# Two projections of a chunk in one visit of the matrix engine, the second result held in SBUF

## The chip, the cores and the metric

The kernel runs on one core of a Trainium2 chip. A core has a matrix engine (TensorE; PE in the rows, PEld for its weight loads), VectorE (DVE), ScalarE (ACT), GpSimd (POOL), and a queue engine (SP) that starts DMA transfers. PE writes only to PSUM, a small memory of eight banks; DVE and ACT read PSUM and SBUF. Each engine takes its instructions strictly in the order in which the program lists them. The metric is the device time in microseconds of one execution.

## The reference

Three stages follow each other: an attention through 32 packed tokens per head, a mixture of 4 experts, and a last two-layer block.

```python
def sm_attn(qq, kk, vv):
    s = scale * np.matmul(qq, kk.transpose(0, 1, 3, 2))
    ...                                   # softmax over the last axis
    return np.matmul(a, vv)
p_packed = sm_attn(p, k, v)               # 4 batch, 8 heads, 32 packed, 64
out = sm_attn(q, p_packed, p_packed)      # 4 batch, 8 heads, 576 tokens, 64
x = out.transpose(0, 2, 1, 3).reshape(2304, 512)
p = domain_probs / (domain_probs.sum(-1, keepdims=True) + 1e-09)
for e in range(4):
    h = np.maximum(x @ w1[e], 0.0)        # 512 -> 1024
    out += p[:, e:e + 1] * (h @ w2[e])    # 1024 -> 512
h = x @ w_in                              # 512 -> 2048
return (h - np.tanh(h)) @ w_out
```

## The kernel before

**What a projection is.** The attention's output x is a product a2 · p_packed, where a2 holds the second softmax (8 heads x 32 packed = 256 numbers per token). So x @ w1 is computed as a2 · (p_packed @ w1). The inner product p_packed @ w1 is the *packed projection* (`pack_w1`, line 528): for one batch element and one chunk of the hidden layer it gives a 256 x 512 weight matrix, by which the 576 tokens of that batch element are then multiplied.

**Tiling.** The expert stage works in two passes `p` over two batch elements each (1152 tokens, 9 tiles of 128). In a pass it goes through 8 chunks `c` (expert c // 2, 512 of its 1024 hidden columns). Per chunk and batch element `bi` there are:

- one projection on PE: 8 matmuls of 64 x 32 weights and 512 columns into the PSUM tile `wps` (line 533); they use the array as eight small tiles side by side. Each is fp32 and is recorded as two passes, so 16 matmul rows in the trace;
- its sums (lines 545 to 557, shared between ACT and DVE): `wps` is split into a high and a low part, and five linear combinations of its quarters are formed in the tile `wsum` and split too. The result `wp` holds seven slots, high and low;
- seven products on PE (`up_prod`, line 612) in four steps, a Winograd scheme, into two PSUM tiles called X and Z (`hpx` and `hpz`, matmuls on line 628); DVE adds (`done`, line 639) and ACT copies (`kept`, line 635) combine them into the hidden values `h0`, `h1` (high and low parts, lines 564 and 565).

The down-projection (`down`, line 670, PSUM tile `yps`, matmuls on line 678) of the hidden values of one token tile is placed between the steps of the products.

**The order.** PE's and SP's orders are written out by hand as strings of tokens; DVE's and ACT's are set by a scheduler at build time. For each chunk there is an *even half* (`EVEN`, products of the first batch element, `g...0` to `g...3`, with five down-projections `d` of the chunk before between them) and an *odd half* (`ODD`, products of the second, with four). In the kernel before, each half ends with one projection for the next chunk: token `W..0` at the end of the even half, `W..1` at the end of the odd half. Background tokens `_` decode the last stage's 64-bit weights on ACT, DVE and POOL at the same time (tiles `f64`, `fo`, `fh`; fetched by SP, line 387).

**Buffers.** `wps` has one buffer of two PSUM banks (pool `psw`). X and Z share two such buffers (pool `ps2`). The raw weights of a chunk come by DMA as two tiles `wraw` (tokens `a0..0` and `a0..1` at the start of the even half), in a pool of two; a reload waits until the projections of the chunk before have read them. `wsum` shares a pool of five with the decoding tiles.

Of the kernel before, what the change touches and what calls it, by code (L numbers as in the profile page):

```python
# [9 lines left out]
F32 = mybir.dt.float32  # L10
F32R = mybir.dt.float32r
U32 = mybir.dt.uint32
ACTF = mybir.ActivationFunctionType
# [57 lines left out]
)  # L71

FIRST = (
    "d005 g1000 Q10 J10 R10 d006 g1001 b10 Q11 J11 R11 L3 d007 a020 a021 g1002 b11 g1003 W200 d008 "
    "g1010 d100 Q12 J12 R12 g1011 d101 Q13 J13 R13 g1012 d102 Q14 J14 R14 k10 k11 a120 a121 g1013 W201 b20 b21 d103 "
)

EVEN = (
    "d%(l)d%(p)d4 _ g%(c)d%(p)d00 a0%(e)d0 a0%(e)d1 _ k%(c)d0 d%(l)d%(p)d5 _ g%(c)d%(p)d01 d%(l)d%(p)d6 _ "
    "k%(c)d1 g%(c)d%(p)d02 _ d%(l)d%(p)d7 g%(c)d%(p)d03 W%(e)d%(q)d0 _ d%(l)d%(p)d8 "  # L80
)

ODD = (
    "g%(c)d%(p)d10 a1%(e)d0 _ d%(c)d%(p)d0 _ g%(c)d%(p)d11 b%(e)d0 _ d%(c)d%(p)d1 a1%(e)d1 _ g%(c)d%(p)d12 "
    "d%(c)d%(p)d2 g%(c)d%(p)d13 W%(e)d%(q)d1 _ d%(c)d%(p)d3 b%(e)d1 _ "
)

LASTA = (
# [21 lines left out]
def kernel(  # L110
# [13 lines left out]
    nc = tc.nc  # L124
# [6 lines left out]
    def pool(name, bufs=1, stack=None, **kw):  # L131
        return (stack or ctx).enter_context(
            tc.tile_pool(name=name, bufs=bufs, **kw, **({} if kw.get('space') == DRAM else {'reuse_waits': 'tile'}))
        )
# [14 lines left out]
    ps2 = pool("ps2", 2, pps, space=PSUM)  # L149
# [17 lines left out]
    psw = []  # L167
# [4 lines left out]
    def k4t(shape, dt, name):  # L172
        return p_k4.tile(shape, dt, tag="k", name=name)
# [8 lines left out]
    def f(ap):  # L182
        return ap.bitcast(F32)
# [119 lines left out]
    def q_scores(p, t0):  # L303
# [20 lines left out]
        sc3 = sc[:, 0:n].rearrange("p (g k) -> p g k", k=32)  # L324
        nc.vector.tensor_reduce(out=mx[:, 0:G, 0], in_=sc3, op=ALU.max, axis=AX.X)
        a2s[p, t0] = n, G, sc3, mx
# [11 lines left out]
    def q_norm(p, t0):  # L338
        a2, a23, G = a2s[p, t0]
        sm = small.tile([128, 16, 1], F32, tag="qsm", name="qsm")  # L340
        nc.vector.tensor_reduce(out=sm[:, 0:G, 0], in_=a23, op=ALU.add, axis=AX.X)
        nc.vector.tensor_scalar(
# [147 lines left out]
    w2h, w2l, wph, wpl, raw, w2s, unsaved = {}, {}, {}, {}, {}, {}, {}  # L490
# [33 lines left out]
    def save_w2(c, g):  # L524
        for k, t in enumerate(unsaved.pop((c, g), ())):
            nc.sync.dma_start(out=w2s[c, g][:, k], in_=f(t))

    def pack_w1(c, p, bi):
        ps = (psw[0] if psw else ps2).tile([128, 2, 512], F32, tag="pw" if psw else "p2", name="wps")
        for j in range(4):  # L530
            for r in range(2):
                d = slice(64 * r, 64 * r + 64)
                nc.tensor.matmul(  # L533
                    out=ps[32 * j:32 * j + 32, r, :],
                    lhsT=ppbd[p][d, bi, j, 32 * r:32 * r + 32], rhs=raw[0, c, j // 2][d, j % 2, :],
                )
        if c == 0:
            w = p_wp.tile([128, 2, 2, 512], F32R, tag="wp", name="wp")
            h, l = wph[c, p, bi], wpl[c, p, bi] = w[:, 0], w[:, 1]
            nc.scalar.activation(out=h, in_=ps, func=ACTF.Copy)  # L540
            nc.vector.tensor_tensor(out=l, in0=ps, in1=f(h), op=ALU.subtract)
            return
        w = p_wp.tile([128, 2, 7, 256], F32R, tag="wp", name="wp")
        h, l = wph[c, p, bi], wpl[c, p, bi] = w[:, 0], w[:, 1]
        s = k4t([128, 4, 256], F32, "wsum")
        a11, a12, a21, a22 = ps[:, 0, 0:256], ps[:, 1, 0:256], ps[:, 0, 256:512], ps[:, 1, 256:512]
        nc.scalar.activation(out=h[:, 0:2], in_=ps[:, :, 0:256], func=ACTF.Copy)
        nc.scalar.activation(out=s[:, 3], in_=a21, func=ACTF.Copy)
        nc.vector.tensor_tensor(out=l[:, 0:2], in0=ps[:, :, 0:256], in1=f(h[:, 0:2]), op=ALU.subtract)
        nc.scalar.activation(out=h[:, 2], in_=a22, func=ACTF.Copy)  # L550
        nc.vector.tensor_tensor(out=s[:, 0], in0=a22, in1=s[:, 3], op=ALU.add)
        nc.vector.tensor_tensor(out=l[:, 2], in0=a22, in1=f(h[:, 2]), op=ALU.subtract)
        nc.vector.tensor_tensor(out=s[:, 1], in0=s[:, 0], in1=a11, op=ALU.subtract)
        nc.vector.tensor_tensor(out=s[:, 2], in0=a11, in1=s[:, 3], op=ALU.subtract)
        nc.vector.tensor_tensor(out=s[:, 3], in0=a12, in1=s[:, 1], op=ALU.subtract)
        nc.scalar.activation(out=h[:, 3:7], in_=s, func=ACTF.Copy)
        nc.vector.tensor_tensor(out=l[:, 3:7], in0=s, in1=f(h[:, 3:7]), op=ALU.subtract)
# [4 lines left out]
    def split_h(fp, d, src):  # L562
        hi, lo = ht[fp]
        last[1] = nc.scalar.activation(out=hi[:, :, d], in_=src, func=ACTF.Relu).ins
        last[0] = nc.vector.scalar_tensor_tensor(
            out=lo[:, :, d], in0=src, scalar=0.0, in1=f(hi[:, :, d]), op0=ALU.max, op1=ALU.subtract,
        ).ins

    def up(c, p, un):
        bi, t0, n = UN[un]  # L570
        if not ht:
            ht.extend([p_h.tile([128, 2, TP * 128], F32R, name=f"h{fp}{s}") for s in "hl"] for fp in range(2))
        for fp in range(2):
            ps = ps2.tile([128, 2, 512], F32, tag="p2", name="hps")
            for ff in range(2):
                c0 = 128 * (2 * fp + ff)
                k = 0
                for g in range(2):
                    for a, x in ((wph, a2h), (wph, a2l), (wpl, a2h)):
                        nc.tensor.matmul(  # L580
                            out=ps[:, ff, 0:n],
                            lhsT=a[c, p, bi][:, g, c0:c0 + 128],
                            rhs=x[p][:, g, t0:t0 + n],
                            start=(k == 0), stop=(k == 5),
                        )
                        k += 1
            split_h(fp, slice(t0, t0 + n), ps[:, :, 0:n])
# [24 lines left out]
    def up_prod(c, p, bi, step):  # L612


        W, t0 = (wph[c, p, bi], wpl[c, p, bi]), bi * S_LEN
        A, T = (a2h[p], a2l[p]), (th[p], tl[p])

        def tok(g, half):
            return [x[:, g, t0 + half * HB:t0 + half * HB + HB] for x in A]

        def cmb(k):
            return [x[:, bi, k] for x in T]

        def mul(ps, slot, x, start, stop):
            for ff in range(2):
                c0 = slice(128 * ff, 128 * ff + 128)
                for k, (a, b) in enumerate(((0, 0), (0, 1), (1, 0))):
                    nc.tensor.matmul(  # L628
                        out=ps[:, ff, 0:HB], lhsT=W[a][:, slot, c0], rhs=x[b],
                        start=(start and k == 0), stop=(stop and k == 2), skip_group_check=True,  # L630
                    )

        def kept(ps, name):
            t = p_ct.tile([128, 2, HB], F32, tag="ct", name=name)
            last[1] = nc.scalar.activation(out=t, in_=ps[:, :, 0:HB], func=ACTF.Copy).ins
            return t

        def done(ps, t, fp, half):
            nc.vector.tensor_tensor(out=t, in0=ps[:, :, 0:HB], in1=t, op=ALU.add)  # L639
            split_h(fp, slice(t0 + half * HB, t0 + half * HB + HB), t)  # L640

        if step == 0:
            X = ps2.tile([128, 2, 512], F32, tag="p2", name="hpx")
            Z = ps2.tile([128, 2, 512], F32, tag="p2", name="hpz")
            mul(X, 0, tok(0, 0), True, False)
            t = kept(X, "p1")
            mul(Z, 1, tok(1, 0), True, True)
            done(Z, t, 0, 0)
            prod[bi] = [X, Z]
        elif step == 1:  # L650
            X, Z = prod[bi]
            mul(X, 4, cmb(1), False, False)
            prod[bi].append(kept(X, "u2"))
            mul(Z, 3, cmb(0), True, False)
            prod[bi].append(kept(Z, "p5"))
        elif step == 2:
            X, Z, u, p5 = prod[bi]
            mul(X, 5, cmb(2), False, False)
            done(X, p5, 1, 1)
            mul(Z, 6, tok(1, 1), False, True)  # L660
            done(Z, u, 0, 1)
        else:
            X = prod.pop(bi)[0]
            mul(X, 2, cmb(3), False, True)
            split_h(1, slice(t0, t0 + HB), X[:, :, 0:HB])
# [257 lines left out]
    def late_norm():  # L923
# [24 lines left out]
        "J": lambda p, i: q_exp(p, 2 * i),  # L948
        "k": save_w2,
        "W": pack_w1,  # L950
        "u": lambda c, p, i: up(c, p, ("u0", "m0", "m1", "u3")[i]),
        "d": down,
        "g": up_prod,
        "C": comb,
        "q": x_quad,
# [279 lines left out]
```

## Time and profile before

| | |
|---|---|
| median of 3 runs (lowest, highest) | 1070.21 us (1069.99, 1071.28) |
| the profiled execution, its own time | 1069.74 us |
| its span, first to last instruction | 1068.0 us |
| chain that ended last, share of PE | 90% |
| of it matmuls of `yps` / `ops` / `h3ps` | 33% / 19% / 16% |
| of it `hpx` / `hpz` / `wps` | 7% / 6% / 3% |

A busy time is the time in which an engine works on at least one instruction; a row of a timeline gives start and duration of one instruction or of several equal ones. Matmuls overlap in their pipeline, so what one costs is the distance from its start to the start of the next, not its duration. A wait names the engine and the instruction that ended it.

### The profile page before, as it was taken

Reading aid. Unit: us, or ns where it says so; the run is one execution under the profiler, and the core shown is the slowest. Engines: PE = TensorE matmul, PEld = TensorE weight load, DVE = VectorE, ACT = ScalarE, POOL = GpSimd, SP = SyncE. Lnnn points to the kernel's source line nnn. Section 1 sums busy time; section 2 is a strip of 40 time slices with the busy share of each in tenths; the row PEclk is TensorE's granted clock in tenths of the full one; section 3 lists DMA queues with packets and bytes.
Section 4 is the critical chain, followed back from the end, with each engine's and each line's share of the span. In section 5 each row is a group of like instructions: output and inputs, shape, how many; then the busy total and the mean of one; then the engine's idle time right before and its main releaser. Section 6 shows DMA issues by size and latency. Waiting matters only on the chain.

```text
span 1068.0 us, 16484 instructions
## 1 busy us (share of the span) xinstructions
PE 1055.8 (99%) x6344; PEld 898.7 (84%) x6344; DVE 884.1 (83%) x1353; ACT 623.9 (58%) x986; POOL 160.4 (15%) x122
## 2 busy tenths in 40 slices
PE   8999999999999999999999999999999999999998
PEld 6777888888888888888888888889999999999897
DVE  4777889989998775798889866788998899898887
ACT  3445545654554346445444443587877788777775
POOL 0000023333434102242424210000000000000000
PEclk9999999999999999999999999999999999999999
DMA  9736427647545653564373342444545644564542
GB/s 341 233 95 241 165 105 246 210 140 248 210 131 188 236 177 114 172 207 146 131 246 139 126 161 95 152 182 173 217 178 195 229 172 155 216 241 162 199 149 99
DMA packets 57727, 192.75 MB, mean 180 GB/s; under 512 B 6448, under 2 KB 8752, under 8 KB 54576
## 3 DMA queue, kind: packets, MB, share of 16 engines
q1 hardware_dynamic: 57648, 191.69, 50.7%
q8 instruction: 50, 0.82, 0.3%
q14 instruction: 29, 0.24, 0.1%
HBM read 144.74 MB, written 46.92 MB: 179 GB/s over the span
## 4 chain that ended last, share of the span: by engine, by line
PE 90%; DVE 6%; ACT 2%; issue 1%; DMA 0%; SPq 0%; ACTq 0%; DVEq 0%
PE yps L678 33%; PE ops L1085 19%; PE h3ps L870 16%; PE hpx L628 7%; PE hpz L628 6%; PE wps L533 3%; PE hps L580 2%; PE pv L293 1%; PE qsc L315 1%; PE sc L237 1%; DVE w2l L520 1%; DVE x L689 1%; DMA kt<-in_kT_dram 0%; PE xps L785 0%; DVE xl L187 0%
## 5 line engine op out<-in xcount | busy, mean ns | idle before, releaser
L1085 PE MATMUL ops<-wo,gh 128*128 128x512 f32 x576 | 178.7, 391 | 0.0
L689 DVE SCALAR_TENSOR_TENSOR x<-yps,pn,x 128x512 f32<-128x512 f32 x126 | 93.7, 744 | 39.5 <-PE yps L678 39.0
L1085 PEld LDWEIGHTS ops<-wo,gh 128*128 128x128 f32 x576 | 107.1, 188 | 20.1 <-ACT gh L1130 0.4
L678 PE MATMUL yps<-w2h,h0h 128*128 128x512 f32 x288 | 117.0, 406 | 0.2 <-DVE x L689 0.2
L1085 PE MATMUL ops<-wo,gl 128*128 128x512 f32 x288 | 113.4, 394 | 0.0
L678 PE MATMUL yps<-w2h,h0l 128*128 128x512 f32 x288 | 113.2, 393 | 0.0
L678 PE MATMUL yps<-w2l,h0h 128*128 128x512 f32 x288 | 112.8, 392 | 0.0
L678 PE MATMUL yps<-w2h,h1h 128*128 128x512 f32 x288 | 112.8, 392 | 0.0
L678 PE MATMUL yps<-w2h,h1l 128*128 128x512 f32 x288 | 112.4, 390 | 0.0
L678 PE MATMUL yps<-w2l,h1h 128*128 128x512 f32 x288 | 112.1, 389 | 0.0
L870 PE MATMUL h3ps<-xh,wg 128*128 128x384 f32 x384 | 106.5, 337 | 0.4 <-ACT h L880 0.4
L418 POOL TENSOR_TENSOR fo<-fo,f 128x512 f32<-128x512 f32 x32 | 46.0, 1440 | 352.7 <-DVE f L414 282.6
L628 PE MATMUL hpx<-th,wp 128*128 128x288 f32 x336 | 81.1, 297 | 0.8 <-DVE p L639 0.8
L678 PEld LDWEIGHTS yps<-w2h,h0h 128*128 128x128 f32 x288 | 54.0, 187 | 31.4 <-issue 21.0
L880 ACT ACTIVATE h<-h3ps 128x384 f32<-128x384 f32 x96 | 46.8, 489 | 51.1 <-PE h3ps L870 50.9
L870 PEld LDWEIGHTS h3ps<-xh,wg 128*128 128x128 f32 x384 | 70.2, 188 | 2.0 <-ACT h L880 0.7
L870 PE MATMUL h3ps<-xl,wg 128*128 128x384 f32 x192 | 64.5, 336 | 0.2 <-DVE xl L187 0.2
L678 PEld LDWEIGHTS yps<-w2h,h1l 128*128 128x128 f32 x288 | 54.1, 188 | 12.0
L678 PEld LDWEIGHTS yps<-w2h,h0l 128*128 128x128 f32 x288 | 54.0, 188 | 12.1
L678 PEld LDWEIGHTS yps<-w2l,h1h 128*128 128x128 f32 x288 | 54.1, 188 | 11.9
L678 PEld LDWEIGHTS yps<-w2h,h1h 128*128 128x128 f32 x288 | 54.1, 188 | 11.6
L1085 PEld LDWEIGHTS ops<-wo,gl 128*128 128x128 f32 x288 | 54.0, 188 | 11.6 <-DVE gl L1068 0.2
(183 smaller groups left out, 2575.0 us busy)
## 6 DMA issues: line engine op xcount, KB each, us to landing
wg<-wing SPq DMA_DIRECT2D x24, 1792.0 KB, 7.6
wraw<-in_w_dram SPq DMA_DIRECT2D x48, 512.0 KB, 5.6
wo<-wout SPq DMA_DIRECT2D x48, 512.0 KB, 8.8
w2s<-w2h SPq DMA_DIRECT2D x16, 512.0 KB, 7.3
w2s<-w2l SPq DMA_DIRECT2D x16, 512.0 KB, 7.5
f<-in_win_dram SPq DMA_DIRECT2D x16, 512.0 KB, 6.9
f<-in_wout_dram SPq DMA_DIRECT2D x16, 512.0 KB, 6.1
wing<-f SPq DMA_DIRECT2D x32, 256.0 KB, 4.6
```

Of the source, the lines that this page charges most:

```text
L237: nc.tensor.matmul(out=sc[64 * jj:64 * jj + 64, h, 0:288], lhsT=pbd[:, 4 * b + j, :], rhs=kv_k[b][j][:, 288 * h:288 * h + 288],)
L293: nc.tensor.matmul(out=pv[64 * h:64 * h + 64, jj, :], lhsT=kv_v[b][c][0:n, 128 * j + 64 * h:128 * j + 64 * h + 64], rhs=a1t[:, c, k0:k0 + ...
L315: nc.tensor.matmul(out=sc[r - r0:r - r0 + 64, 256 * i:256 * i + 256].rearrange("p (r j k) -> p r j k", r=2, j=4)[:, :, j, :], lhsT=qs[2 * ...
L418: nc.gpsimd.tensor_tensor(out=lf, in0=lf, in1=st[:, :, 1].bitcast(F32), op=ALU.mult)
L533: nc.tensor.matmul(out=ps[32 * j:32 * j + 32, r, :], lhsT=ppbd[p][d, bi, j, 32 * r:32 * r + 32], rhs=raw[0, c, j // 2][d, j % 2, :],)
L580: nc.tensor.matmul(out=ps[:, ff, 0:n], lhsT=a[c, p, bi][:, g, c0:c0 + 128], rhs=x[p][:, g, t0:t0 + n], start=(k == 0), stop=(k == 5),)
L628: nc.tensor.matmul(out=ps[:, ff, 0:HB], lhsT=W[a][:, slot, c0], rhs=x[b], start=(start and k == 0), stop=(stop and k == 2), skip_group_che ...
L678: nc.tensor.matmul(out=ps, lhsT=a[:, ff, o:o + 128], rhs=w[c, fp][:, ff], start=(k == 0), stop=(k == 11),)
L689: last[0] = nc.vector.scalar_tensor_tensor(out=x2[tt], in0=ps, scalar=pn[:, tt, e:e + 1], in1=x2[tt], op0=ALU.mult, op1=ALU.add,).ins
L870: nc.tensor.matmul(out=ps, lhsT=wg[n][:, a, slot, 128 * kk:128 * kk + 128], rhs=x[c][b][kk] if isinstance(x[c][b], list) else x[c][b][:, k ...
L880: nc.scalar.activation(out=hs[n][a][b], in_=xz[n]["XZ".index(i)], func=ACTF.Copy)
L1085: nc.tensor.matmul(out=ps, lhsT=a, rhs=wo[n][ff][:, w], start=(i == 0 and ff == 0 and k == 0), stop=(i == NG - 1 and ff == 1 and k == 2), ...
```

## The change

Both projections of a chunk are issued at the end of the even half, one behind the other (token `y`, `pack_pair`). The first goes to `psw` as before. The second goes to a buffer of the pool `ps2`, that of X and Z; an ACT copy of 128 x 1024 moves it, unsplit, into the SBUF tile `wraw` that held the first half of the chunk's raw weights. The sums of the second one stand in the program at the end of the odd half as before (token `p`, `pack_held`), but now read that SBUF tile and not PSUM. X and Z are allocated in the other order in the even half. The pair stands at 13 places: one in the opening (`FIRST`), six in each pass; the projections of the start and of the turn between the passes stay single.

```diff
--- before.py
+++ after.py
...
-    "k%(c)d1 g%(c)d%(p)d02 _ d%(l)d%(p)d7 g%(c)d%(p)d03 W%(e)d%(q)d0 _ d%(l)d%(p)d8 "
+    "k%(c)d1 g%(c)d%(p)d02 _ d%(l)d%(p)d7 g%(c)d%(p)d03 y%(e)d%(q)d _ d%(l)d%(p)d8 "
-    "d%(c)d%(p)d2 g%(c)d%(p)d13 W%(e)d%(q)d1 _ d%(c)d%(p)d3 b%(e)d1 _ "
+    "d%(c)d%(p)d2 g%(c)d%(p)d13 p%(e)d%(q)d _ d%(c)d%(p)d3 b%(e)d1 _ "
...
@@ -525,8 +525,25 @@
         for k, t in enumerate(unsaved.pop((c, g), ())):
             nc.sync.dma_start(out=w2s[c, g][:, k], in_=f(t))
 
+    held = {}
+
+    def pack_pair(c, p):
+
+        ps = pack_mm1(c, p, 0)
+        two = pack_mm1(c, p, 1, ps2)
+        held[c, p] = raw[0, c, 0]
+        nc.scalar.activation(out=held[c, p], in_=two, func=ACTF.Copy)
+        pack_sums(c, p, 0, ps)
+
+    def pack_held(c, p):
+        pack_sums(c, p, 1, held.pop((c, p)))
+
     def pack_w1(c, p, bi):
-        ps = (psw[0] if psw else ps2).tile([128, 2, 512], F32, tag="pw" if psw else "p2", name="wps")
+        pack_sums(c, p, bi, pack_mm1(c, p, bi, psw[0] if psw else ps2))
+
+    def pack_mm1(c, p, bi, pl=None):
+        pl = pl or psw[0]
+        ps = pl.tile([128, 2, 512], F32, tag="p2" if pl is ps2 else "pw", name="wps")
         for j in range(4):
             for r in range(2):
                 d = slice(64 * r, 64 * r + 64)
@@ -534,6 +551,9 @@
                     out=ps[32 * j:32 * j + 32, r, :],
                     lhsT=ppbd[p][d, bi, j, 32 * r:32 * r + 32], rhs=raw[0, c, j // 2][d, j % 2, :],
                 )
+        return ps
+
+    def pack_sums(c, p, bi, ps):
         if c == 0:
             w = p_wp.tile([128, 2, 2, 512], F32R, tag="wp", name="wp")
             h, l = wph[c, p, bi], wpl[c, p, bi] = w[:, 0], w[:, 1]
@@ -640,8 +660,11 @@
             split_h(fp, slice(t0 + half * HB, t0 + half * HB + HB), t)
 
         if step == 0:
-            X = ps2.tile([128, 2, 512], F32, tag="p2", name="hpx")
-            Z = ps2.tile([128, 2, 512], F32, tag="p2", name="hpz")
+            X, Z = (
+                ps2.tile([128, 2, 512], F32, tag="p2", name=k) for k in (("hpz", "hpx"), ("hpx", "hpz"))[bi]
+            )
+            if bi == 0:
+                X, Z = Z, X
             mul(X, 0, tok(0, 0), True, False)
             t = kept(X, "p1")
             mul(Z, 1, tok(1, 0), True, True)
@@ -948,6 +971,8 @@
         "J": lambda p, i: q_exp(p, 2 * i),
         "k": save_w2,
         "W": pack_w1,
+        "y": pack_pair,
+        "p": pack_held,
         "u": lambda c, p, i: up(c, p, ("u0", "m0", "m1", "u3")[i]),
         "d": down,
         "g": up_prod,
```

What moves on PE at the end of an even half of the first pass (before, then changed; `wps_2855` is the projection of the first batch element, `hpx` the last product, `yps` the next down-projection):

```order
L628 MATMUL hpx_2725<-th_947,wp_2496 128x288
L533 MATMUL wps_2855<-wraw_2744,ppbd_209 32x512 x4
L533 MATMUL wps_2855<-wraw_2746,ppbd_209 32x512 x4
L678 MATMUL yps_2880<-w2h_2221,h0h_442 128x512
L678 MATMUL yps_2880<-w2l_2222,h0h_442 128x512
```

```order
L648 MATMUL hpx_2730<-th_947,wp_2509 128x288
L550 MATMUL wps_2859<-wraw_2748,ppbd_209 32x512 x4
L550 MATMUL wps_2859<-wraw_2750,ppbd_209 32x512 x4
L550 MATMUL wps_2868<-wraw_2748,ppbd_209 32x512 x4
L550 MATMUL wps_2868<-wraw_2750,ppbd_209 32x512 x4
L701 MATMUL yps_2894<-w2h_2233,h0h_442 128x512
L701 MATMUL yps_2894<-w2l_2234,h0h_442 128x512
```

A second group of eight (`wps_2868`) now stands between the first one and the down-projection.

On PE at the end of the odd half that follows, where the second batch element's projection was `wps_3023`:

```order
L628 MATMUL hpx_2894<-th_947,wp_2662 128x288
L533 MATMUL wps_3023<-wraw_2744,ppbd_209 32x512 x4
L533 MATMUL wps_3023<-wraw_2746,ppbd_209 32x512 x4
L678 MATMUL yps_3050<-w2h_2586,h0h_442 128x512
L678 MATMUL yps_3050<-w2l_2587,h0h_442 128x512
```

```order
L648 MATMUL hpx_2908<-th_947,wp_2666 128x288 x2
L648 MATMUL hpx_2908<-tl_948,wp_2666 128x288
L648 MATMUL hpx_2908<-th_947,wp_2666 128x288
L701 MATMUL yps_3055<-w2h_2599,h0h_442 128x512
L701 MATMUL yps_3055<-w2l_2600,h0h_442 128x512
```

The projection is gone, and the down-projection follows the product directly.

On ACT behind the visit at the end of that even half (`wp` the split weights, `p1`, `h0h` the next half's products):

```order
L548 ACTIVATE wsum_2865<-wps_2855 128x256
L550 ACTIVATE wp_2864<-wps_2855 128x256
L635 ACTIVATE p1_2902<-hpx_2894 128x576
L564 ACTIVATE h0h_442<-p1_2902 128x2x288
L556 ACTIVATE wp_2864<-wsum_2865 128x1024
L635 ACTIVATE u2_2944<-hpx_2894 128x576
```

```order
L568 ACTIVATE wsum_2879<-wps_2859 128x256
L570 ACTIVATE wp_2878<-wps_2859 128x256
L535 ACTIVATE wraw_2748<-wps_2868 128x1024
L576 ACTIVATE wp_2878<-wsum_2879 128x1024
L655 ACTIVATE p1_2916<-hpx_2908 128x576
L568 ACTIVATE wsum_3038<-wraw_2748 128x256
L584 ACTIVATE h0h_442<-p1_2916 128x2x288
L655 ACTIVATE u2_2958<-hpx_2908 128x576
```

The copy into `wraw` stands behind the third instruction of the first element's sums; the last one, L576 (L556 before), and the first of the held tile's sums moved ahead of `h0h`.

## Rows read from the trace of the kernel before

**Rows 1.** The page: busy time by engine; a DMA's us to landing.

```profile
PE 1055.8 (99%) x6344; PEld 898.7 (84%) x6344; DVE 884.1 (83%) x1353; ACT 623.9 (58%) x986; POOL 160.4 (15%) x122
...
f<-in_win_dram SPq DMA_DIRECT2D x16, 512.0 KB, 6.9
```

**Rows 2.** Busy us per engine, summed over 142.72:335.70 and 415.87:607.94.

```profile
sum 385.05, PE 383.55 PEld 318.10 DVE 338.42 ACT 196.57 POOL 138.93; mean PE 191.78 PEld 159.05 DVE 169.21 ACT 98.29 POOL 69.47
```

**Rows 3.** Timeline of PE: start us, us, engine, line, operation, tiles, shape.

```profile
415.65 0.29 PE L628 MATMUL hpx<-th,wp 128*128 128x288 f32 x1
...
416.89 0.50 PE L678 MATMUL yps<-w2h,h0h 128*128 128x512 f32 x1
417.22 0.39 PE L678 MATMUL yps<-w2l,h0h 128*128 128x512 f32 x1
...
429.88 0.30 PE L628 MATMUL hpz<-a2h,wp 128*128 128x288 f32 x1
430.01 0.39 PE L678 MATMUL yps<-w2h,h0h 128*128 128x512 f32 x1
430.24 0.39 PE L678 MATMUL yps<-w2l,h0h 128*128 128x512 f32 x1
```

**Rows 4.** PE's timeline in two narrow windows: the two passes of one projection.

```profile
415.87 0.66 PE L533 MATMUL wps<-wraw,ppbd 64*32 64x512 f32 x8
...
416.32 0.64 PE L533 MATMUL wps<-wraw,ppbd 64*32 64x512 f32 x8
```

**Rows 5.** DVE's timeline before that projection: the add that frees Z's buffer.

```profile
412.43 0.76 DVE L639 TENSOR_TENSOR u<-hpz,u 128x576 f32<-128x576 f32 x1
```

**Rows 6.** What touches the projection's tile: ns min/median/max of one.

```profile
L540 ACT ACTIVATE wp<-wps x4: 1008/1022/1024, 19.5 to 355.3; 128x1024 fp32r<-128x1024 f32 x4
...
L549 DVE TENSOR_TENSOR wp<-wps,wp x28: 672/690/694, 76.8 to 627.8; 128x512 fp32r<-128x512 f32 x28
```

**Rows 7.** Timeline of ACT in two late halves: L550 of the projection's sums.

```profile
262.90 0.39 ACT L550 ACTIVATE wp<-wps 128x256 fp32r<-128x256 f32 x1 [0.76 <-DVE wp L549]
...
573.86 0.39 ACT L550 ACTIVATE wp<-wps 128x256 fp32r<-128x256 f32 x1 [2.28 <-DVE wp L549]
```

**Rows 8.** Timeline of PE in the same halves: product Z starts.

```profile
262.20 0.29 PE L628 MATMUL hpz<-a2h,wp 128*128 128x288 f32 x1
...
573.62 0.29 PE L628 MATMUL hpz<-a2h,wp 128*128 128x288 f32 x1
```

**Rows 9.** Groups by line and shape: xcount, busy us, mean ns, idle us.

```profile
L557 DVE TENSOR_TENSOR wp<-wsum,wp 128x1024 fp32r<-128x1024 f32 x28 | 35.7, 1277 | 8.2 <-ACT wp L556 8.0
...
L565 DVE SCALAR_TENSOR_TENSOR h0l<-u,h0h 128x576 fp32r<-128x576 f32 x28 | 28.5, 1019 | 0.3
...
L565 DVE SCALAR_TENSOR_TENSOR h1l<-p,h1h 128x576 fp32r<-128x576 f32 x28 | 25.4, 909 | 0.7
...
L565 DVE SCALAR_TENSOR_TENSOR h0l<-p,h0h 128x576 fp32r<-128x576 f32 x28 | 23.1, 825 | 6.5 <-ACT h0h L564 6.5
...
L565 DVE SCALAR_TENSOR_TENSOR h1l<-hpx,h1h 128x576 fp32r<-128x576 f32 x28 | 21.0, 750 | 6.2 <-ACT h1h L564 6.0
...
L541 DVE TENSOR_TENSOR wp<-wps,wp 128x1024 fp32r<-128x1024 f32 x4 | 4.9, 1218 | 0.6 <-ACT wp L540 0.6
```

**Rows 10.** Line 565, ns min/median/max: SBUF source, then PSUM source.

```profile
L565 DVE SCALAR_TENSOR_TENSOR h0l<-u,h0h x28: 743/758/1855, 101.2 to 662.3; 128x576 fp32r<-128x576 f32 x28
L565 DVE SCALAR_TENSOR_TENSOR h1l<-hpx,h1h x28: 740/748/759, 103.0 to 667.6; 128x576 fp32r<-128x576 f32 x28
```

**Rows 11.** Waits of PE for DVE adds: us in total, times, longest.

```profile
PEld hpx L628 <- DVE p L639: 1.5, 2, 1.2
...
PEld hpz L628 <- DVE p L639: 1.2, 2, 0.7
```

**Rows 12.** Timeline of SP: the fetch behind the reload of the raw weights.

```profile
435.63 0.42 SPq L387 DMA_DIRECT2D f<-in_win_dram  x1
```

**Rows 13.** Timeline of ACT: the instruction that reads that fetch.

```profile
444.11 0.66 ACT L394 ACTIVATE fo<-f 128x512 f32<-128x512 uint32 x1
```

More of the change, by code (lines that the diff above doesn't have):

```diff
@@ L73 @@
 FIRST = (
-    "d005 g1000 Q10 J10 R10 d006 g1001 b10 Q11 J11 R11 L3 d007 a020 a021 g1002 b11 g1003 W200 d008 "
-    "g1010 d100 Q12 J12 R12 g1011 d101 Q13 J13 R13 g1012 d102 Q14 J14 R14 k10 k11 a120 a121 g1013 W201 b20 b21 d103 "
+    "d005 g1000 Q10 J10 R10 d006 g1001 b10 Q11 J11 R11 L3 d007 a020 a021 g1002 b11 g1003 y20 d008 "
+    "g1010 d100 Q12 J12 R12 g1011 d101 Q13 J13 R13 g1012 d102 Q14 J14 R14 k10 k11 a120 a121 g1013 p20 b20 b21 d103 "
 )
```

## The prediction

> **What bounds the kernel now.** I read the page first: matmuls (PE) are busy 1055.8 of the 1068.0 us, VectorE (DVE) 83%, ScalarE (ACT) 58% [rows 1]. The reader is to see that PE has nothing to wait for, so time is won only by shortening what PE itself does, and lost by anything that makes it wait. The stage that changes is the expert stage, and the windows of its steady halves show the same at closer range: in 385.05 us PE is busy 383.55, DVE 338.42 (88%), GpSimd (POOL) 138.93 (36%) [rows 2]. DVE has 12% to spare, in a queue that runs strictly in order. Then the timeline of PE around one projection visit, which is what the change merges, and last the rows of ACT and DVE that free the buffers into which PE writes next.
>
> **What one visit costs.** At 415.65 the last matmul of a product starts, and the next thing on PE is the projection: 8 matmuls of 64x512 at 415.87, 8 more at 416.32 (each fp32 matmul is recorded as two passes), then the down-projection at 416.89 and its second matmul at 417.22 [rows 3, 4]. Without a projection between, a product's last matmul is followed by the down-projection after 0.13 us (429.88 to 430.01), and that one's second matmul after another 0.23 (430.24) [rows 3]. So the visit costs 417.22 - 415.65 - 0.13 - 0.23 = 1.21 us. Of this the eight tiles really stream for two passes of 416.32 - 415.87 = 0.45 each, 0.90 us; the other 0.31 us is spent on getting into and out of the small-tile form: the first projection matmul starts 0.22 and not 0.13 after its predecessor, the down-projection starts only when the tiles run dry, and its second matmul comes after 0.33 and not 0.23.
>
> **The change, part by part.** (1) *One visit fewer per chunk.* At the end of the odd half PE goes straight from the product to the down-projection: minus 1.21 us. At the end of the even half 16 more passes stand behind the first 16. They use the same eight tiles in the same order, so the nearest row for the step from one group to the next is the step from pass to pass, 0.45: plus 0.90. Bounds: nothing is gained but 0.19 if the second group must wait until the first has run dry (416.89 - 415.87 = 1.02 us, rows 4), and no row gives a reason for a group to cost more than a whole visit of 1.21. I take 0.90. The token strings put a pair at 13 places (one in the opening, six in either pass over the chunks), so 13 x (1.21 - 0.90) = 4.0 us, between 0 and 4.0 with 2.5 for 0.19.
>
> (2) *The buffer of the second group.* It is the one that the even half's product Z has just left, free when DVE has done the add u<-hpz. That add ran at 412.43 for 0.76, 2.7 us before the visit [rows 5]: no wait.
>
> (3) *Thirteen copies of 128x1024 on ACT*, priced by the nearest row, a 128x1024 copy out of PSUM, at 1.02 us [rows 6]: 13.3 us on an engine at 58%. Their place is what counts. The order puts the copy behind L550 of the first element's sums, and L550 waits for DVE (L549). Until the copy has run, PE cannot start product Z of the odd half in that buffer. Where DVE is late, that is too late: in one half L550 ends at 262.90 + 0.39 = 263.29, the copy would end at 264.31, and Z, which started at 262.20, will be due 0.90 later, at 263.10: PE waits 1.2 us. In another L550 ends at 574.25, the copy at 575.27, and Z (573.62) is due at 574.52: 0.75 us [rows 7, 8]. I looked at all 13 places; these are the two where the copy is clearly late. Cost 1.95 us; bounds 0 (ACT runs the copy before L550, as it may in some halves) and 13 x 1.02.
>
> (4) *The second element's sums read SBUF instead of PSUM, and earlier.* Six DVE instructions per chunk (the subtractions and sums of L549 to L555), in 12 chunks (chunk 0 has one). Their bare time does not change: 128x1024 from PSUM 1218 ns, from SBUF 1277 [rows 9]. What changes is what else they meet. DVE instructions of one shape, 128x576, take 750 ns on average with one source in PSUM and never over 759; with both in SBUF they take 825, 909 and 1019 on average and up to 1855 [rows 9, 10]; the same sum from PSUM, L549, never exceeds 694 [rows 6]. So an instruction with two SBUF sources is sometimes held up, by 269, 159, 75 and 59 ns on average in these four rows, mean 140. That gives 6 x 12 x 0.14 = 10.1 us more DVE time, in halves where DVE has about 12% idle. How much of it reaches PE? The 28 instances of those four forms lose 28 x (0.269 + 0.159 + 0.075 + 0.059) = 15.7 us now, and PE waits for DVE's adds 2.7 us in all [rows 11]: 0.17 us for each. I take 10.1 x 0.17 = 1.7 us; bounds 0 and 10.1.
>
> The Trainium skill has a rule that speaks here, in "GPSIMD Engine Reference", section 8, Key points: GpSimd shares its SBUF interfaces with VectorE, and a VectorE instruction with two SBUF inputs contends with it. The trace agrees: only the forms with two SBUF sources show the long instances. By the rule every sum moved off PSUM is exposed; if sources in SBUF were as good as in PSUM, this term would be 0 and the total 1.7 us lower.
>
> (5) *Relief.* With the sums of the second element done from the held tile while the odd half runs, the burst behind the odd visit is shorter. Of PE's 2.7 us of waits for adds, the two at product Z (1.2 us) come in even halves, behind exactly those sums; I let them go: minus 1.2. The other group (1.5 us) is in the odd and even halves where DVE is full; part of it falls in the half that already waits for the copy, so minus 0.6.
>
> (6) *Loads.* The tile of the first raw weights is now free only when the held sums have read it, some 2 us later than before. Queued behind its reload on SP stands a fetch, issued at 435.63, landing after 6.9 us at about 442.5, read by ACT at 444.11 [rows 1, 12, 13]. Two us later it is late by about 0.4 us on ACT, which is not what PE waits for there. Nothing.
>
> **The sum.** -4.0 + 1.95 + 1.7 - 1.2 - 0.6 = about -2.2 us. The profiled execution took 1069.74 us (span 1068.0 and 1.74 around it), so it would take 1067.6; the median of the runs is 0.47 above it, so 1068.0 us.
>
> **Rivals.** *The clean gain.* ACT and DVE run the new work early enough and neither (3) nor (4) reaches PE: 1070.2 - 4.0 - 0 to 1.8 = 1064.4 to 1066.2. For it: DVE's idle 12% and the new order, in which the first element's six sums stand close together. Against it: the two late halves are a fact of the trace of before, and their cause (DVE held up) does not go.
>
> *The switch is not saved*: the second group waits until the first has drained, 0.19 per pair, 2.5 us in place of 4.0: 1069.5. For it: the down-projection behind a visit does wait in that way. Against: the second pass of each tile does not, and the second group is in the same form as the first.
>
> *The held sums crowd DVE* (the other side). Four of the six sums now stand among the odd half's own adds, ahead of the ones that free product X for its last step. If three quarters of the 10.1 us reach PE, the total is -4.0 + 1.95 + 7.6 - 1.8 = +3.75: 1074.0. It takes the whole gain from 3.85 us on, 38% of the added DVE time, and 0.2% beyond that from 6.0 us, 59%. For it: DVE at 88%, in order. Against: today only 17% of such delay reaches PE.
>
> That the change does not do what it says (the second group kept waiting by its buffer) is ruled out by (2) as far as the trace can tell.
>
> **Chances.** Forecast, part of the gain given back, 1066.5 to 1069.5: 0.45. Clean gain 0.22, switch not saved 0.13, crowding 0.20. A difference of 0.2%, 2.1 us, is about the least that a measurement of this kernel tells from none: the borders are 1068.1 and 1072.4. The forecast lies on the first, so it gives 0.24 faster and 0.21 same; the clean gain is faster; the unsaved switch 0.02 and 0.11; crowding 0.17 slower and 0.03 same. Faster 0.48, same 0.35, slower 0.17. The range from 1064.8 to 1072.0 leaves out the end of the clean gain and most of the crowding.
>
> **What would show it.** (1): after a pair, 32 projection passes whose third group of eight starts 0.90 after the first; if it starts at 1.02, the switch is not saved; at the odd half's end the down-projection 0.13 after the product. (3): PE idle before product Z of the odd half, ended by the ACT copy, in one to three halves. (4): the sums reading the held tile with a mean above 0.45 us and single instances over 1 us; PE's waits for adds near 3 us in all. If these waits reach 6 us, the forecast is wrong on the slow side; if neither copies nor adds are waited for, on the fast side.

## The result, and the profile after

The changed kernel is slower: 1076.57 us (median of 6 runs, 1074.6 to 1078.27) against 1070.38 us (6 runs) on the same chip, ratio 1.0060, 95% interval 1.0050 to 1.0069. The profiled execution took 1074.6 us, 4.9 more than that of before; in it the granted clock is full. The other five had mean clocks of 0.996 to 0.999 and took 0.8 to 3.7 us longer; experiment 1 shows a likely cause.

The page of the changed kernel, busy time by engine and the chain that ended last by engine, answers to [rows 1]; the third line is the chain of the kernel before:

```profile
PE 1054.5 (98%) x6344; PEld 900.2 (84%) x6344; DVE 890.8 (83%) x1353; ACT 636.7 (59%) x999; POOL 163.8 (15%) x122
...
PE 80%; DVE 12%; ACT 3%; issue 2%; DMA 1%; POOL 1%; SPq 0%; DVEq 0%; ACTq 0%; POOLq 0%
...
PE 90%; DVE 6%; ACT 2%; issue 1%; DMA 0%; SPq 0%; ACTq 0%; DVEq 0%
```

PE is 1.3 us less busy, but the chain now runs through DVE for 12% of the span instead of 6%. DVE is 6.7 us busier, though it does the same 1353 instructions on the same shapes.

The merged visit on PE's timeline (start us, us, engine, line, operation, tiles, shape), first at the end of an even half, then at the end of an odd one; it answers to [rows 3]:

```profile
420.85 0.29 PE L648 MATMUL hpx<-th,wp 128*128 128x288 f32 x1
421.08 1.95 PE L550 MATMUL wps<-wraw,ppbd 64*32 64x512 f32 x32
422.96 0.50 PE L701 MATMUL yps<-w2h,h0h 128*128 128x512 f32 x1
423.29 0.39 PE L701 MATMUL yps<-w2l,h0h 128*128 128x512 f32 x1
...
439.53 0.29 PE L648 MATMUL hpx<-th,wp 128*128 128x288 f32 x1
439.67 0.40 PE L701 MATMUL yps<-w2h,h0h 128*128 128x512 f32 x1
```

The down-projection starts 422.96 - 421.08 = 1.88 us after the first pass, where a single visit took 1.02 [rows 4]: the second group costs 0.86, and at the odd half's end the down-projection starts 0.14 after the product, where 0.13 was forecast. PE's side of the change is what was predicted. What PE waits for is not. The waits (waiter, line, what ended the wait: us in total, times, longest) answer to [rows 11]. PEld is the weight load in front of a matmul, so a PEld row and the PE row of the same name are the same waits. The last line is of the kernel before:

```profile
PEld yps L701 <- DVE x L712: 6.0, 6, 2.3
PE yps L701 <- DVE x L712: 4.2, 6, 1.9
PEld hpz L648 <- DVE p L659: 2.0, 3, 1.0
PEld hpz L648 <- ACT wraw L535: 1.8, 2, 1.6
...
PEld yps L678 <- DVE x L689: 0.4, 1, 0.4
```

In the first row the down-projection of the next token tile waits for DVE's update `x` (L712), which frees `yps`; before, there was one such wait of 0.4 us. Measured by the distance between starts of matmuls, PE loses about 9.5 us from 95 to 650 us, against 2.5 before: about 5.2 behind `x` (0.3 before), 1.9 behind DVE's adds (2.2), 1.5 behind the ACT copy and 1.0 behind `h1l` (none before).

Why DVE is late is seen where a wait arises. DVE's timeline (the stretch that ends in a late `x`):

```profile
202.65 1.86 DVE L585 SCALAR_TENSOR_TENSOR h0l<-u,h0h 128x576 fp32r<-128x576 f32 x1
204.43 0.74 DVE L585 SCALAR_TENSOR_TENSOR h1l<-hpx,h1h 128x576 fp32r<-128x576 f32 x1
205.10 1.11 DVE L569 TENSOR_TENSOR wp<-wraw,wp 128x512 fp32r<-128x512 f32 x1
206.13 1.52 DVE L572 TENSOR_TENSOR wp<-wraw,wp 128x256 fp32r<-128x256 f32 x1
207.57 0.74 DVE L712 SCALAR_TENSOR_TENSOR x<-yps,pn,x 128x512 f32<-128x512 f32 x1
```

and POOL's at the same time, then PE's waits:

```profile
202.41 3.26 POOL L419 TENSOR_TENSOR fo<-fo,f 128x512 f32<-128x512 f32 x2
205.63 1.74 POOL L438 TENSOR_TENSOR fo<-fo,fh 128x512 fp32r<-128x512 f32 x1
...
205.23 0.50 PE L701 MATMUL yps<-w2h,h1l 128*128 128x512 f32 x1 [0.83 <-DVE h1l L585]
208.37 0.50 PE L701 MATMUL yps<-w2h,h0h 128*128 128x512 f32 x1 [0.36 <-DVE x L712]
```

L572 takes 0.41 us when nothing is in its way. It starts at 206.13, half a microsecond into POOL's L438 (205.63 to 207.37), and ends at 207.65, 0.28 after POOL has ended. L569 before it, 0.68 us when alone, likewise ends 0.54 after the L419 in which it started (205.67). `h1l<-hpx` and `x`, with one source in PSUM, run in 0.74 beside the same POOL instructions. Of the 27 `h0l<-u` from 95 to 650 us, the 16 that meet no POOL instruction take at most 0.76 us, the 11 that do 1.29 on average. So a DVE instruction with both sources in SBUF that comes while a POOL instruction runs stands until that one has ended. This is called a hold below. The two places of the same line show it in all instances (the tile view, ns min/median/max):

```profile
L569 DVE TENSOR_TENSOR wp<-wps,wp x16: 678/692/693, 76.7 to 615.4; 128x512 fp32r<-128x512 f32 x16
L569 DVE TENSOR_TENSOR wp<-wraw,wp x12: 675/681/1784, 125.1 to 633.0; 128x512 fp32r<-128x512 f32 x12
...
L572 DVE TENSOR_TENSOR wp<-wraw,wp x12: 410/416/1516, 125.7 to 633.6; 128x256 fp32r<-128x256 f32 x12
```

From PSUM the longest is 693 ns, from the held tile 1784, at the same median. The Trainium skill says this in "SBUF — State Buffer", section "SBUF: two separate sides": the port pair that VectorE and GpSimd share is an exclusive lock, held for a whole instruction, and the other engine is blocked until its end. The trace agrees: L572 loses 1.1 us, not a part of its bandwidth.

### The profile page after: what moved, and what is told of

Its sections match the earlier page's. It is cut to its first block, busy times and chain, and to the rows that moved or that the text cites. A ratio compares the mean times of both kernels' runs of the same rounds, so it can differ in the third digit from the quotient of the medians.

```text
span 1072.6 us, 16453 instructions
## 1 busy us (share of the span) xinstructions
PE 1054.5 (98%) x6344; PEld 900.2 (84%) x6344; DVE 890.8 (83%) x1353; ACT 636.7 (59%) x999; POOL 163.8 (15%) x122
## 4 chain that ended last, share of the span: by engine, by line
PE 80%; DVE 12%; ACT 3%; issue 2%; DMA 1%; POOL 1%; SPq 0%; DVEq 0%; ACTq 0%; POOLq 0%
PE yps L701 27%; PE ops L1110 19%; PE h3ps L893 16%; PE hpx L648 6%; PE hpz L648 5%; PE wps L550 2%; PE hps L600 2%; PE pv L293 1%; DVE x L712 1%; DVE h0l L585 1%; DVE h1l L585 1%; DMA f<-in_win_dram 1%; DVE p L659 1%; DVE w2l L520 1%; DVE f L410 1%
## 5 line engine op out<-in xcount | busy, mean ns | idle before, releaser
L712 DVE SCALAR_TENSOR_TENSOR x<-yps,pn,x 128x512 f32<-128x512 f32 x126 | 93.7, 745 | 43.1 <-PE yps L701 42.8
L418 POOL TENSOR_TENSOR fo<-fo,f 128x512 f32<-128x512 f32 x32 | 47.3, 1480 | 346.4 <-DVE f L414 277.8
```

Of the source, the lines that this page charges most:

```text
L418: nc.gpsimd.tensor_tensor(out=lf, in0=lf, in1=st[:, :, 1].bitcast(F32), op=ALU.mult)
L712: last[0] = nc.vector.scalar_tensor_tensor(out=x2[tt], in0=ps, scalar=pn[:, tt, e:e + 1], in1=x2[tt], op0=ALU.mult, op1=ALU.add,).ins
```

## The experiments

Every run is set against the kernel before on the same chip. Two theories stood at the start: P, that the order of DVE's queue does the harm (held sums ahead of adds and updates that PE needs), and C, that being held up by POOL does, whatever the order.

**1. The held sums late.**

```diff
-        pack_sums(c, p, 1, held.pop((c, p)))
+        with tc.issue_after(last[0]), tc.issue_after(last[1]):
+            pack_sums(c, p, 1, held.pop((c, p)))
```

> The pair is kept; only the sums of the held tile may not be placed ahead of the last step of the odd half's product any more, so on DVE they stand where the second projection's sums stood before the change. Theory P (placement: early held sums stand ahead of the adds and of the x updates for which PE waits): PE's waits for DVE (x updates, h1l, adds; 7 us now) fall back to the 2.5 us of the kernel before, the copy's 1.5 us stays; 1070.4 - 3.6 + 1.5 + 0.5 = about 1069. Theory C (two sources in SBUF make the sums longer, and that reaches PE wherever they stand): waits stay at 6 us or more, 1073 to 1077.

Measured: 1080.33 us, ratio 1.0094 (1.0080 to 1.0108): 10.4 us above the kernel before, where the change itself is 6.2 above it, and above the ranges of both theories. P's repair makes it worse, so P alone cannot be the main cause. In the new place the held sums met POOL more often; five of the six had instances over 1.5 us, three in the changed kernel, and PE waited for the copy longer, 4.2 us and not 1.8. Four of the five in the tile view:

```profile
L572 DVE TENSOR_TENSOR wsum<-wraw,wsum x12: 409/418/1529, 124.9 to 638.5; 128x256 f32<-128x256 f32 x12
L575 DVE TENSOR_TENSOR wsum<-wraw,wsum x12: 408/416/1514, 125.2 to 638.9; 128x256 f32<-128x256 f32 x12
L573 DVE TENSOR_TENSOR wp<-wraw,wp x12: 408/415/1528, 125.6 to 639.2; 128x256 fp32r<-128x256 f32 x12
L574 DVE TENSOR_TENSOR wsum<-wsum,wraw x12: 410/412/1529, 127.7 to 640.6; 128x256 f32<-128x256 f32 x12
```

DVE's busy time is 898.3 us, 7.5 more than in the changed kernel. This run also shows what a long wait costs behind it. PE's windows around one of 1.9 us that ended at 325.17 (us, then busy time and count of PE, PEld, DVE, ACT, POOL, then the granted clock, DMA share, GB/s):

```profile
322.00:324.90 2.90, 1.26 (x6) 0.72 (x4) 2.87 (x4) 2.55 (x6) 1.23 (x1) 1.00 0.88 316
327.00:328.00 1.00, 1.00 (x3) 0.73 (x3) 1.00 (x4) 0.00 (x0) 0.00 (x0) 0.50 0.17 66
329.00:330.00 1.00, 1.00 (x7) 0.87 (x6) 1.00 (x3) 0.00 (x0) 0.00 (x0) 1.00 0.00 0
```

PE runs at half clock, 1.2 GHz, for some 3 us after it; eight matmuls start 0.38 or 0.43 us apart and not 0.23 to 0.24, together 1.5 us. The profiled execution of the changed kernel has a wait as long at the same place (from 322.02) and keeps its clock, while its five other runs have lower mean clocks. Such stretches would account for the median: a mean clock of 0.998 is 0.002 x 1074 = 2.1 us of clock lost, and the two runs with 0.998 took 1.7 and 2.2 us longer than the profiled one. Where in those runs the clock was low, no trace shows.

**2. Late, and the second element's projection first.**

```diff
-        ps = pack_mm1(c, p, 0)
-        two = pack_mm1(c, p, 1, ps2)
+        two = pack_mm1(c, p, 1, ps2)
+        ps = pack_mm1(c, p, 0)
```

> As the kernel with the late held sums, and within the pair the second element's projection comes first, so that the ACT copy can start 0.9 us earlier and stands ahead of the first element's sums. Theory P with the copy as the second cost: the wait of product Z for the copy (1.5 us in one place) goes too; about 1067 to 1068, 1 to 1.5 us below the kernel without this edit. If the copy is no cost: the same as without it. The first element's sums start 0.9 us later; if these are late for the odd half's products, slower by 1 to 3 us.

Measured: 1075.83 us, 1.0055 (1.0042 to 1.0067), 4.5 us below experiment 1. There PE had waited for the copy in four places, 4.2 us by the row `hpz <- ACT wraw`; here that row is gone. The expectation of 1067 to 1068 was missed. The copy's place is a real cost, but with late sums and the copy out of the way 5.9 us above the kernel before are left: two waits for `x` of 5.6 us together are the largest part, waits for adds another.

**3. The sums from SBUF alone, without pairs.** In the kernel before, at the end of the odd half:

```diff
+        if bi == 1 and c and psw and (c, p) != (0, 1):
+            nc.scalar.activation(out=raw[0, c, 0], in_=ps, func=ACTF.Copy)
+            ps = raw[0, c, 0]
```

> The kernel before, unpaired, with one thing of the change: the second projection's result is copied by ACT into the tile of the raw weights, and its sums read that tile instead of PSUM; their place stays at the end of the odd half. Theory C: the six sums take 40 to 170 ns more each, DVE busy +6 to +7 us, and PE's waits rise by about as much: 1074 to 1077. Theory P: the sums lengthen as much, but PE's waits stay near 2.5 us: 1070 to 1072 (the sums start 1.0 us later behind the copy).

Measured: 1072.46 us, 1.0025 (1.0015 to 1.0035). DVE's busy time rose by 6.1 us (890.2 against 884.1), as both theories said, and the time by 2.5, between the two expectations. PE's waits rose from 2.5 to only about 4 us, and none of them is for `x` beyond the 0.4 us of before. So nearly the same holds as in the changed kernel cost much less where the sums stand late and no pair is in front of them: the place of a hold decides how much of it reaches PE. In this the order has a share, which was not taken apart.

**4. Pairs in the second pass only.** In the opening (`FIRST`) and in the loop over the chunks; the `p` tokens go back to single projections likewise (not shown):

```diff
-    "... g1002 b11 g1003 y20 d008 "
+    "... g1002 b11 g1003 W200 d008 "
...
-            run(EVEN % w if w["q"] < 2 else LASTA)
+            run((EVEN if w["q"] == 1 else EVEN.replace('y%(e)d%(q)d', 'W%(e)d%(q)d0')) % w if w["q"] < 2 else LASTA)
```

> The change in the second pass over the chunks alone (six pairs); the first pass and the opening keep the single projections. In the traces the first pass lost 5.2 us with the change and the second gained 0.3. If the loss is that of the first pass, where DVE also splits the second weights: 1069 to 1070, at best 6 x 0.28 = 1.7 us below the kernel before (1068.7). If the cost comes with any pair, whatever else DVE has to do: above 1071.

Measured: 1070.04 us, 1.0003 (0.9994 to 1.0012), just above the first expectation. The loss belongs to the first pass; in the second the gain of 6 x 0.28 = 1.7 us is spent on two waits for `x` (1.1 and 0.6 us) and one of 0.5 for the copy.

**5 and 6. Both kernels nearly without POOL.** In each, the three decode lines of POOL work on 8 columns and leave the rest undecoded (one line of the three is shown):

```diff
-        nc.gpsimd.tensor_tensor(out=lf, in0=lf, in1=st[:, :, 0].bitcast(F32), op=ALU.add)
+        nc.gpsimd.tensor_tensor(out=lf[:, 0:8], in0=lf[:, 0:8], in1=st[:, 0:8, 0].bitcast(F32), op=ALU.add)
```

> The kernel before, with GpSimd's decode instructions cut from 512 or 256 columns to 8 (the last stage's weights are then not decoded in full), as the control for the changed kernel with the same cut. Without GpSimd beside them DVE's instructions with two SBUF sources should show no instance above 0.8 us (128x576). PE's waits of 2.5 us mostly go: 1067 to 1069.

> The changed kernel with the same cut of GpSimd's work. Theory C (what slows the changed kernel is GpSimd beside DVE's instructions with two SBUF sources, now six more per chunk): the sums from the held tile take their bare 410 to 690 ns, PE's waits for DVE (7 us) go, and the pair's gain appears: 2 to 3.6 us below the control, the copy's wait taken off. Theory P (order of DVE's queue, whatever GpSimd does): still 3 us or more above the control.

Measured: before 1068.10 us, 0.9987 (0.9979 to 0.9996); changed 1065.01, 0.9957 (0.9945 to 0.9970). The change, which costs 6.2 us, gains 3.1 with POOL out of the way. The pages, before and changed:

```profile
PE 1054.8 (99%) x6344; PEld 898.7 (84%) x6344; DVE 850.2 (80%) x1353; ACT 625.0 (59%) x986; POOL 33.0 (3%) x122
```

```profile
PE 1051.4 (99%) x6344; PEld 899.9 (85%) x6344; DVE 849.5 (80%) x1353; ACT 637.9 (60%) x999; POOL 38.1 (4%) x122
```

DVE's busy time is now the same in both. Against the full kernels the holds are 884.1 - 850.2 = 33.9 us before and 890.8 - 849.5 = 41.3 us changed. The sums of the held tile now cost what they cost from PSUM (the tile view of the changed kernel), and one wait for `x` is left (the last line):

```profile
L574 DVE TENSOR_TENSOR wsum<-wraw,wsum x12: 416/419/421, 109.6 to 608.5; 128x256 f32<-128x256 f32 x12
...
L569 DVE TENSOR_TENSOR wp<-wraw,wp x12: 675/681/690, 125.5 to 623.3; 128x512 fp32r<-128x512 f32 x12
...
PEld yps L701 <- DVE x L712: 0.9, 1, 0.9
```

All of PE's waits for the copy are gone too. In the changed kernel it was late because ACT, ahead of it, waited for a held DVE: ahead of the late copy ACT stands 2.23 us for L399, which takes 1.66 us there and never more than 0.71 in experiment 6. This is C: without the holds the order of the change does no harm. That the cut also finishes the decoded weights earlier is not the reason: in the changed kernel no wait of DVE is ended by POOL, and ACT waits for POOL 7.0 us in all, 9.2 before.

**7 and 8. Four held sums on POOL**, which can read SBUF (7), and that with the second projection first (8). One of the four; `eng` is `nc.gpsimd` for the held tile:

```diff
-        nc.vector.tensor_tensor(out=s[:, 0], in0=a22, in1=s[:, 3], op=ALU.add)
+        eng.tensor_tensor(out=s[:, 0], in0=a22, in1=s[:, 3], op=ALU.add)
```

> The changed kernel with four of the six held sums (those that form wsum) on GpSimd instead of DVE, which only the SBUF tile allows. DVE loses 12 x (0.51 + 0.45 + 0.51 + 0.49) = 23.5 us; GpSimd gains 48 instructions of about 0.8 us. If DVE's load in the odd half is what PE waits for: waits for x, h1l and adds fall from 7 to under 3 us, the copy's 1.5 us stays: 1068 to 1071. If contention with GpSimd is the cost: the 38 us more on GpSimd lengthen other DVE instructions by as much as is saved: 1073 to 1077.

> As the kernel with four held sums on GpSimd, and the second element's projection first within the pair, so that the copy is done before product Z needs the buffer. If both costs are then gone: 1066.5 to 1068, faster than the kernel before. If contention is the cost: 1072 or more.

Measured: 1074.80 us, 1.0048 (1.0035 to 1.0061), and 1075.92, 1.0059 (1.0045 to 1.0072). DVE should lose 23.5 us and loses 890.8 - 880.1 = 10.7; more than half comes back as holds of its other instructions. One of the four sums on POOL, 256 columns:

```profile
L575 POOL TENSOR_TENSOR wsum<-wraw,wsum 128x256 f32<-128x256 f32 x12 | 15.6, 1299 | 0.9
```

Its mean (the last number but one) is 1299 ns where L574 of the same shape takes 799: 11 of the 12 start while a DVE instruction with its sources in SBUF runs, of L574 only 2. The hold works both ways: in the changed kernel the 18 L418 on POOL that start beside no such instruction take 1.31 us (at most 1.32), the other 14 1.70. Both kernels end where the second expectation put them; that the second projection first gains nothing here, and 4.5 us in experiment 2, is explained in part by the trace: the waits for the copy (2.1 us) are gone, but those for `x` grew from 4.9 to 7.5 us. Why they grew is left open, as the edit also changes DVE's order.

**9, 10 and 11. POOL's instructions in quarters**: in the changed kernel (9), in the kernel before (10), and changed with the second projection first (11). One of the three decode lines:

```diff
-        nc.gpsimd.tensor_tensor(out=parts[name][1], in0=f(t), in1=f(h), op=ALU.subtract)
+        for a in range(0, t.shape[-1], 128):
+            d = slice(a, a + 128)
+            nc.gpsimd.tensor_tensor(out=parts[name][1][:, d], in0=f(t)[:, d], in1=f(h)[:, d], op=ALU.subtract)
```

> The changed kernel, each of GpSimd's decode instructions cut into pieces of 128 columns (448 instead of 128 instructions on POOL, the same work). Theory C in its sharp form (a DVE instruction with two SBUF sources that comes while a GpSimd instruction runs waits to the end of that one instruction): the longest instance of the held sums falls from 1.0 to 1.1 us above its bare time to about 0.5, DVE's busy time falls by 15 to 25 us, PE's waits from 9.5 to under 4: 1067 to 1070. Rival (DVE is held as long as GpSimd has work at all, or the pieces' own overhead eats it): no instance gets shorter, 1074 or more.

> The kernel before with the same cut into quarters, the control: DVE's busy time falls by 15 to 20 us, PE's waits from 2.5 to about 1: 1068 to 1069.5. Rival (overhead of the pieces): 1070 to 1072.

> The changed kernel with GpSimd in quarters, and the second element's projection first in the pair. If what is left of the waits in the version without this edit is the copy: 0.5 to 1.5 us below it; about 1066 to 1068, faster than the kernel before. If DVE has enough room there, the copy is in time anyway: the same within 0.5 us.

Measured: 1072.44 us, 1.0024 (1.0014 to 1.0034); 1068.19, 0.9990 (0.9981 to 0.9998); 1067.77, 0.9983 (0.9974 to 0.9991). That a hold lasts one POOL instruction is borne out; in experiment 9 (the line numbers are 4 higher; a piece takes POOL 0.56 to 0.61 us):

```profile
L573 DVE TENSOR_TENSOR wp<-wraw,wp x12: 673/684/954, 125.4 to 629.9; 128x512 fp32r<-128x512 f32 x12
L576 DVE TENSOR_TENSOR wp<-wraw,wp x12: 413/421/687, 126.0 to 630.5; 128x256 fp32r<-128x256 f32 x12
```

The longest is 0.27 us above the median, where the expectation said about 0.5. DVE's busy time falls to 867.0. But the time of experiment 9 missed its expectation of 1067 to 1070. POOL now needs 238.6 us for its work instead of 163.8 and is late itself, which makes the longest wait. ACT's timeline there, and a window (columns as in experiment 1) behind that wait:

```profile
202.21 1.05 ACT L580 ACTIVATE wp<-wsum 128x1024 fp32r<-128x1024 f32 x1
208.76 0.63 ACT L434 ACTIVATE fh<-fo 128x512 fp32r<-128x512 f32 x1 [5.50 <-POOL fo L421]
...
210.44 0.63 ACT L434 ACTIVATE f<-fo 128x512 fp32r<-128x512 f32 x1 [0.50 <-POOL fo L421]
210.98 0.63 ACT L659 ACTIVATE p<-hpx 128x576 f32<-128x576 f32 x1
...
213.50:216.00 2.50, 2.50 (x8) 2.02 (x8) 2.38 (x4) 2.10 (x4) 1.41 (x4) 0.50 1.02 403
```

`p<-hpx`, for which PE stands 2.0 us, is queued behind two decode copies that wait for POOL. Behind that wait the granted clock is 0.50 for some 3 us, which costs about 1.7 us more, and three waits for `x` remain (2.7 us). Experiment 10 came out as expected: DVE is busy 862.7 us, and PE's waits are under 1 us. Experiment 11 is the fastest kernel that decodes all the weights: 0.17% below the kernel before and, with overlapping intervals, 0.4 us below experiment 10. It is 4.7 us below experiment 9, far more than the 0.5 to 1.5 that was expected and more than the copy, which cost 0.2 there. By the traces 2.4 us of it are fewer waits (3.1 against 5.5, by the distance between starts) and 1.7 the half clock; why the waits are fewer was not taken apart, as the edit also orders DVE anew. It still loses 2.8 us to experiment 6, which has no holds: its DVE is busy 868.4 us, and PE stands 1.3 us for ACT's `p` and 0.9 us for an add.

**12. Halves in place of quarters**, the rest as 11 (256 for 128 in the diff above).

> The changed kernel, second projection first, with GpSimd's decode instructions in pieces of 256 columns instead of 128. With quarters (1067.8) POOL took 248 us in all and one wait of 1.5 us came from ACT waiting for POOL's late result ahead of the copy p<-hpx. Halves hold a DVE instruction for up to 0.84 us instead of 0.6, and POOL takes about 180 to 190 us. If POOL's lateness is now the larger cost: 1066 to 1067.5. If the hold of DVE still is: 1069 to 1072.

Measured: 1069.96 us, 0.9995 (0.9986 to 1.0004). POOL takes 202.6 us, DVE 873.7, and PE stands 1.3 us for `h1l` and 0.9 for `x`, for which it hardly waits in experiment 11. So the longer hold is the larger cost. Quarters come out 0.12% better against the kernel before, with intervals that just overlap, so this is likely rather than shown.

## Why the prediction was wrong

The forecast was 1068.0 us, some 2 us less than before; the change cost 6.2 us instead.

**(1) The visit** held: 0.86 us for the second group where 0.90 was forecast. A fifth of the 0.35 us saved is taken back: in experiments 5 and 6 the twelve matmuls behind a pair take 2.87 us and those behind a single visit 2.83, and the odd half's end gains 1.18 us and not 1.21. A chunk without a wait lasts 38.00 us and not 38.28 (windows, before without POOL and then changed without POOL):

```profile
295.83:334.11 38.28, 38.28 (x225) 31.81 (x224) 32.63 (x57) 20.96 (x34) 3.55 (x11) 1.00 0.46 159
...
295.25:333.25 38.00, 38.00 (x225) 31.91 (x225) 32.60 (x57) 21.81 (x35) 4.75 (x11) 1.00 0.50 170
```

So the pairs give 13 x 0.28 = 3.6 us instead of 4.0. **(2)** held as well.

**(4) is the step that failed**, by its share and not by its size. The holds were forecast at 10.1 us; the 72 held sums lost 7.1 us to them in the changed kernel, each counted from the shortest of its line, and DVE as a whole 6.7 to 7.4. The share of 0.17 that reaches PE is what was wrong. It was PE's wait for the adds over the holds of four other DVE forms, averaged over all chunks, and in most chunks DVE has time left: before, it is busy 29.6 to 36.2 us in chunks of 38.28 to 39.31. And it looked at the adds alone, while the held sums stand in front of other work. Of the 7.0 us by which PE's waits grew, 4.9 are for `x` and 1.0 for `h1l`, for which the forecast had no term. That is 5.9 us of wait for about 7 us of hold, a share of about 0.8. The sign that was named, waits for adds near 3 us, did not see this: they came to 2.3 us. One chunk late in the first pass, before and then changed (windows, columns as above):

```profile
296.87:335.70 38.83, 38.53 (x226) 31.84 (x225) 36.23 (x55) 20.80 (x34) 14.87 (x10) 1.00 0.50 164
```

```profile
300.90:341.19 40.29, 38.38 (x226) 31.87 (x225) 37.88 (x57) 21.80 (x35) 14.70 (x10) 1.00 0.52 173
```

The same chunk has 32.6 us of DVE work (57 instructions) in experiments 5 and 6. With the holds it was 36.2 before (55 instructions) and 37.9 changed (57), in a chunk for which PE needs 38.0, so there is next to no room for a further hold. Which share of each single hold reached PE was not measured. Experiment 3 shows that the share is not one number: the same sums from SBUF, late and without pairs, lengthened DVE by 6.1 us and PE's waits by about 1.5.

In all PE's waits grew by 9.5 - 2.5 = 7.0 us, and 7.0 - 3.6 leaves 3.4 of the profiled 4.6 us of span; the rest lies in gaps under 0.12 us each, about 0.2 in most chunks of the first pass, which were not itemized.

**(3) The copy** was sized right (one wait of 1.5 us, forecast 1.95 in two) and its cause named right, DVE held up; yet it was summed beside (4), while experiment 6 shows that both are one cause. **(5) The relief** of 1.8 us came to 0.3 to 0.4: waits for the adds of `hpx` fell from 1.5 to 0.3 us, those of `hpz`, which were to go, rose from 1.2 to 2.0. **(6)** held: counted from the visit, the fetch behind the reload was issued 2.7 us later, and no wait of PE or DVE in this stage is ended by a load.

One reading of the trace was wrong as well. Long instances are not confined to forms with two SBUF sources: L414, which has one, reaches 1414 ns in the kernel before, at a median of 420 (shown in the last section).

The rival "the held sums crowd DVE" named the place and gave 1074.0 for the median, which is 1076.57; the profiled execution took 1074.6. That it comes so near to the latter is in part luck: it let 7.6 us of the holds reach PE, 5.9 did, and it kept the relief of 1.8 us. It also lacked the lower mean clock of the other executions, which took 0.8 to 3.7 us longer, probably by stretches of half clock behind long waits as in experiment 1. Its point of decision was 3.85 us of the holds reaching PE.

## What to carry to other kernels

Before an operand is moved from PSUM to SBUF, look at what POOL does at that time: the DVE instruction's price is then its own time plus what is left of a running POOL instruction, and the longest instance in the trace says more than the mean. Take the share of a delay that reaches the bounding engine from the fullest stretch, not from an average over stretches with room. Long POOL instructions beside a full DVE are worth cutting into pieces as far as POOL has time for their overhead; here it took 1.4 us off the kernel before (experiment 10).

## What the runs showed of the hardware

That the hold lasts to the end of the POOL instruction (1.1 us for L572, at most 0.3 for the held sums with POOL in quarters) and works in both directions (L418 on POOL, 1.31 and 1.70 us) was not in the forecast, which took it as a mean of 0.14 us. It also strikes some instructions with one source, where that and the result lie in SBUF. L414, before and in experiment 6:

```profile
L414 DVE TENSOR_SCALAR f<-f x32: 412/420/1414, 142.7 to 618.3; 128x512 uint32<-128x512 uint32 x32
```

```profile
L414 DVE TENSOR_SCALAR f<-f x32: 418/422/430, 143.3 to 615.2; 128x512 uint32<-128x512 uint32 x32
```

It handles 512 columns in about 420 ns, where L410 with two sources takes 685 there, and is held like the forms with two sources: the three instances over 0.5 us before all start while a POOL instruction runs. A wait of PE of about 2 us can be followed by some 3 us at half clock, in some executions and not in others: it was in the traces of experiments 1, 7, 8 and 9 (waits of 1.9 to 3.0 us), and not in the profiled execution of the changed kernel (1.9 us) nor in that of experiment 2 (2.6 and 2.4 us).
